# Attention and two MoE layers on one core: transposes five units behind the scores, products seven, and a fifth row buffer

## The chip, the cores and the metric

The kernel runs on one core of one Trainium2 chip. The metric is the device time of one execution in microseconds, the median of three runs. One execution was also recorded by the hardware profiler; it has a span (first to last instruction) and a time of its own.

## The reference, cut to what matters

```python
def _attn_ref(q, k, v, f):                       # 4 batches, 8 heads, 576 positions, head_dim 64
    scores = scale * np.matmul(q, k.transpose(0, 1, 3, 2))
    cum = np.cumsum(np.log(np.clip(f, 0.0001, 1.0)), axis=-1)
    decay = cum[:, :, :, None] - cum[:, :, None, :]
    scores = np.where(causal, -1000000000.0, scores + decay)
    attn = np.exp(scores - np.max(scores, axis=-1, keepdims=True))
    attn = attn / (np.sum(attn, axis=-1, keepdims=True) + 1e-09)
    return np.matmul(attn, v)

def reference(...):                              # 2304 tokens of width 512
    x = attn_out.transpose(0, 2, 1, 3).reshape(B * S, H * D)
    x = _moe_ref(x, w_gate, w_val, w_out, rms_g) # rms norm, silu(x@w_gate)*(x@w_val)@w_out, d_ff 1536
    return _moe2_ref(x, w_in, w_out)             # silu(x@w_in)@w_out, d_ff 2048
```

The MoE weights come as float64 and are cut to float32 on the chip.

## The kernel before

The program has two stages that hardly overlap on TensorE: attention first, then the two layers, each matmul of the latter split into three products of high and low parts (`terms`, L754).

Attention works on 16 pairs of heads (`Pair`), and in each pair on nine **units** (`Rows`): unit c holds query block c of both heads in 128 partitions and (c+1)*64 keys. The units of a pair are taken in the order of `ORDER`: c = 0, 1, 7, 2, 6, 3, 5, 4, 8, so that scores of 64, 128, 512, 192, 448, 256, 384, 320 and 576 keys (320 and 256 in two pieces) follow each other. For a unit:

- `bias` (GpSimd, L441 and L443) builds the decay in a tile `dt`;
- `scores` (L454) makes three matmuls into a PSUM bank `s` (four banks); VectorE adds the decay and takes the row extreme (L457) into a row buffer `pr`, which comes from a pool of `PRB` = 4 tiles of 128x576;
- `expo` (ScalarE, L470) applies the exponential in place;
- `turn` (L479, and L486 for the last block) transposes the row on TensorE in up to four pieces and moves it (L272 on ScalarE, L274 on VectorE) into a tile `g`;
- `use`, once in a pair, after unit c = 8, multiplies with v (L510): two groups of matmuls, results `t` and `o`. A matmul here has 64 columns: head j = 0 fills the lower half of the array's columns and j = 1 the upper half, and the loop writes them alternately.

A hand-written loop over steps sets the order of the program: at step s it writes the turn of unit s - `TURN`, the scores and the exponential of unit s, then the use of unit s - `USE`, then jobs that stand in a table by step: loads of a pair 12 steps before its first unit, transposes of k (L413) 6 steps and of q (L413) 5 steps before it, the tails of both (`operand_tails`, L424) 4 steps before it, the row sums of the decay (`load_sums`, L407) 8 steps before it. Jobs of the norm (L297 to L374) follow `USE`. A scheduler then orders each engine's instructions; where one is not ready by its reckoning, a later one of the program can go first. The order it writes is fixed: an engine executes it as it stands.

The weights of the layers are fetched (`weights`, L144) into one of two tiles `st`, cut to float32 into a tile `f`, and split into tiles `wh` and `wl` (`unit_plain`, L189 and L190), four buffers each. The first of them are prepared during attention; `spread` holds the n-th such work until after the exponential of unit 22, 40 and so on (`PLACE`, `STRIDE`).

Of the kernel before, what the change touches and what calls it, by code (L numbers as in the profile page):

```python
# [9 lines left out]
F32 = mybir.dt.float32  # L10
F32R = mybir.dt.float32r
I32 = mybir.dt.int32
# [6 lines left out]
P = 128  # L19
# [8 lines left out]
PRB = 4  # L28
# [3 lines left out]

ORDER = (0, 1, 7, 2, 6, 3, 5, 4, 8)

TURN = 4
USE = 6

WHEN = dict(load=-12, k=-6, sums=-8, q=-5, tails=-4)

# [21 lines left out]
def block_kernel(ctx: ExitStack, tc: tile.TileContext, q, k, v, f, w_gate, w_val, w_o1, rms_g, w_in, w_o2, ident_d, sel_d, hot_d, out):  # L61
    nc = tc.nc
    B, H, S, D = q.shape
    NT, DM = out.shape
# [4 lines left out]
    FULL = NC - 1  # L69
    TAIL = S - FULL * P  # L70
    SF = FULL * P
# [41 lines left out]
    wip = ctx.enter_context(tc.tile_pool(name="wip", bufs=4))  # L113
    wop = ctx.enter_context(tc.tile_pool(name="wop", bufs=3))
    stp = ctx.enter_context(tc.tile_pool(name="stp", bufs=2))
# [10 lines left out]
    def words(w):  # L126
        return (w, 1) if w.dtype == F32 else (w.bitcast(I32), 2)

    def weights(w, src, cols, key):

        n = DM
        wide = src.dtype != F32
        if cols is not None:
            src = src.rearrange("(c p) f -> p c f", p=P)
        if not wide or key in kept:
            if wide:
                nc.sync.dma_start(out=w, in_=kept[key])
            else:
                nc.sync.dma_start(out=w if cols is None else w.rearrange("p (c f) -> p c f", f=cols), in_=src)
            return  # L140
        wi = w.bitcast(I32)
        dst = stp.tile([P, 2 * n], I32, tag="st", name="st")
        pr = dst.rearrange("p (n t) -> p n t", t=2)
        nc.sync.dma_start(out=dst if cols is None else dst.rearrange("p (c f) -> p c f", f=cols), in_=src)  # L144
        top, low = pr[:, :, 1], pr[:, :, 0]
        nc.scalar.activation(out=w, in_=top.bitcast(F32), func=AF.Abs)  # L146
        nc.vector.tensor_scalar(out=w, in0=w, scalar1=FLOOR, scalar2=CAP, op0=ALU.max, op1=ALU.min)
        nc.vector.tensor_scalar(out=wi, in0=wi, scalar1=3, scalar2=0x3FFFFFF8, op0=ALU.logical_shift_left, op1=ALU.bitwise_and)
        nc.vector.scalar_tensor_tensor(out=wi, in0=top, scalar=-0x40000000, in1=wi, op0=ALU.bitwise_and, op1=ALU.bitwise_or)
        nc.vector.scalar_tensor_tensor(out=wi, in0=low, scalar=29, in1=wi, op0=ALU.logical_shift_right, op1=ALU.bitwise_or)  # L150
        kept[key] = dram.tile([P, n], F32, name="kept" + "_".join(map(str, key)))
        nc.sync.dma_start(out=kept[key], in_=w)
# [58 lines left out]
    def attention():  # L211
        exps, maxima = [], []
        with ExitStack() as st:
# [7 lines left out]
            prb = pool("prb", PRB)  # L221
# [154 lines left out]
            class Pair:  # L376
# [7 lines left out]
                def load(self, names="kqv"):  # L384
                    b, hp = self.b, self.hp
                    for nm in names:
                        src = {"k": k, "q": q, "v": v}[nm]
                        t = self.v if nm == "v" else nat.tile([P, NC, 2, D], F32, tag="nqk", name="n" + nm)
                        for j in range(2):
                            nc.sync.dma_start(out=t[:, :FULL, j], in_=src[b, 2 * hp + j, :SF].rearrange("(c p) d -> p c d", p=P))  # L390
                        for i, u in enumerate({"k": (), "q": (q, k), "v": (v,)}[nm]):
                            nc.sync.dma_start(out=t[i * TAIL : (i + 1) * TAIL, FULL], in_=u[b, 2 * hp : 2 * hp + 2, SF:].rearrange("j p d -> p j d"))
                        self.n[nm] = t

                def load_sums(self):

                    b, hp = self.b, self.hp
                    self.nct = t = dec.tile([P, S], F32, tag="ncb", name="ncb", bufs=2)
                    h = b * H + 2 * hp
                    if h == 0:  # L400
                        for w in (slice(0, HS), slice(HS, S)):
                            bp = bank(pss)[:, : w.stop - w.start]
                            nc.tensor.matmul(bp, lhsT=hot, rhs=n8[:, w], start=True, stop=True)
                            nc.scalar.activation(out=t[:, w], in_=bp, func=AF.Copy)
                    else:
                        for j in range(2):
                            nc.sync.dma_start(out=t[j * D : (j + 1) * D], in_=nc8d[h + j, :].partition_broadcast(D))  # L407

                def operand(self, nm):
                    n = self.n[nm]  # L410
# [11 lines left out]
                def operand_tails(self):  # L422
                    tl = bank(pss)
                    nc.tensor.transpose(tl[:, :P], self.n["q"][:, FULL].rearrange("p j d -> p (j d)"), ident)  # L424
                    for j in range(2):
# [2 lines left out]
                        hi, lo = (o[js, at_].rearrange("p (i w) -> p i w", w=w)[:, :, :D] for o in (self.oh, self.ol))  # L428
                        split(hi, lo, tl[js, :P].rearrange("p (i w) -> p i w", w=D))

            class Rows:


# [10 lines left out]

                def scores(self):
                    p, c, n = self.p, self.c, self.n
                    self.pr = prb.tile([P, S], F32, tag="pr", name="pr")
                    cs = slice(c * P, (c + 1) * P)
                    nms = []
                    for k0, w in ((0, n),) if n <= SF else ((0, G2 + D), (G2 + D, G2)):  # L450
                        at_ = QW + k0 + (D if n <= SF else 0)
                        sp = bank(pss)[:, :w]
                        for z, (l, r) in enumerate(((p.oh, p.oh), (p.oh, p.ol), (p.ol, p.oh))):
                            nc.tensor.matmul(sp, lhsT=l[:, cs], rhs=r[:, at_ : at_ + w], start=(z == 0), stop=(z == 2))  # L454
                        nm = sml.tile([P, 1], F32, tag="nm", name="nm", bufs=4)
                        ks = slice(k0, k0 + w)
                        reduced = nc.vector.tensor_tensor_reduce(  # L457
                            out=self.pr[:, ks], in0=sp, in1=self.dt[:, ks], op0=ALU.add, op1=ALU.min, scale=-SCALE, scalar=3.0e38, accum_out=nm
# [89 lines left out]
            nc8d = dram.tile([BH, S], F32, name="nc8d")  # L548
# [28 lines left out]
            nc.sync.dma_start(out=gcol, in_=rms_g.rearrange("(c p) -> p c", p=P))  # L577

            units, jobs = [], {}

            def at(step, *fns):
                jobs.setdefault(step, []).extend(fns)
# [18 lines left out]
            for n, p in enumerate(pairs):  # L601
                s = n * per
# [407 lines left out]
```

## Time and profile before

| | us |
|---|---|
| median of three runs (lowest, highest) | 1029.16 (1027.78, 1029.46) |
| the profiled execution's own time | 1031.82 |
| its span | 1030.0 |
| TensorE shown as busy in the span | 1015.3 |

The profile counts a matmul as busy from its start to a modelled end, so that short waits between matmuls hide in it. What a matmul takes in a stream is better read from start to start in the timeline.

### The profile page before, as it was taken

To read this page: it belongs to the slowest core of one execution; us is meant where nothing else is said; L and a number is where in the kernel's file an instruction comes from. 1 tells how busy PE (TensorE), PEld (TensorE's weight loads), DVE (VectorE), ACT (ScalarE), POOL (GpSimd) and SP (SyncE) were. 2 spreads that over 40 slices of the span, in tenths; PEclk is the share of its full clock that TensorE was granted. 3 is DMA by queue.
4 is the path that set the end of the run, shared out by engine and by line. 5 is a ranking of instruction groups with operands and counts; after the bars stand their busy time and mean duration, and the time that the engine had idled before them with its cause. 6 is when DMAs were issued, how large, how long until landed. Compare 5 with 4: busy or idle time off the path is not lost.

```text
span 1030.0 us, 16062 instructions
## 1 busy us (share of the span) xinstructions
PE 1015.3 (99%) x5457; PEld 849.5 (82%) x5457; DVE 758.2 (74%) x1519; ACT 566.5 (55%) x1193; POOL 395.9 (38%) x589
## 2 busy tenths in 40 slices
PE   8999999999999999999999999999999999999998
PEld 7877888878788888888888887888888888888887
DVE  6889887877788787876588768946666687366664
ACT  6998989884443332543544556564444465544441
POOL 7777656511011135331344633335533323222310
PEclk8999999999999999999999999999999999999999
DMA  6664433123645444230334222223322233121102
GB/s 143 169 185 124 124 93 95 36 63 111 191 148 188 133 151 153 72 123 31 108 123 138 82 62 82 83 82 113 113 83 82 82 123 144 42 62 62 51 1 82
DMA packets 114162, 106.40 MB, mean 103 GB/s; under 512 B 62896, under 2 KB 83792, under 8 KB 114080
## 3 DMA queue, kind: packets, MB, share of 16 engines
q1 hardware_dynamic: 112352, 102.23, 32.6%
q10 hardware_dynamic: 1728, 3.15, 1.0%
q8 instruction: 43, 0.70, 0.3%
q14 instruction: 39, 0.32, 0.1%
HBM read 79.59 MB, written 25.76 MB: 102 GB/s over the span
## 4 chain that ended last, share of the span: by engine, by line
PE 74%; DVE 3%; DMA 1%; ACT 1%; issue 1%; ACTq 0%; SPq 0%; DVEq 0%
PE t L754 38%; PE s L754 19%; PE x L754 16%; DMA c<-t 1%; DVE hl L673 1%; DMA st<-in_moe_w_in_dram 0%; PE o L510 0%; DVE t1l L673 0%; DVE xa L950 0%; PE s L297 0%; DVE b11l L673 0%; DVE c L771 0%; DVE c L885 0%; DVE xa L932 0%; PE t L479 0%
## 5 line engine op out<-in xcount | busy, mean ns | idle before, releaser
L203 POOL TENSOR_TENSOR wol<-c,woh 128x512 fp32r<-128x512 f32 x53 | 77.4, 1467 | 250.3 <-ACT woh L202 224.5
L673 DVE TENSOR_TENSOR hl<-c,hh 128x512 fp32r<-128x512 f32 (+1 forms) x140 | 107.5, 776 | 43.5 <-ACT hh L672 42.7
L165 POOL TENSOR_TENSOR f<-f 128x256 f32<-128x256 f32 x112 | 91.7, 840 | 110.4 <-DMA f<-keptb 64.3
L672 ACT ACTIVATE hh<-c 128x512 fp32r<-128x512 f32 (+1 forms) x140 | 79.6, 583 | 47.6 <-DVE c L885 42.5
L766 ACT ACTIVATE c<-t 128x512 f32<-128x512 f32 x84 | 49.6, 591 | 95.7 <-PE t L754 92.2
L441 POOL TENSOR_SCALAR dt<-ncb,c8t 128x64 f32<-128x64 f32 (+2 forms) x144 | 78.6, 547 | 36.2 <-DVE nm L457 28.3
L878 ACT ACTIVATE c<-c 128x512 f32<-128x512 f32 x66 | 41.6, 630 | 86.7 <-DVE c L771 86.7
L470 ACT ACTIVATE pr<-pr,nm 128x192 f32<-128x192 f32 (+3 forms) x144 | 80.2, 557 | 12.4 <-DVE nm L457 9.0
L457 DVE CUSTOM_DVE_ANT_0 pr<-s,dt 128x256 f32<-128x256 f32 (+7 forms) x160 | 70.1, 450 | 14.9 <-PE t L479 5.2
L190 POOL TENSOR_TENSOR wl<-f,wh 128x1024 fp32r<-128x1024 f32 x12 | 29.2, 2435 | 126.8 <-ACT wh L189 120.5
L171 DVE TENSOR_TENSOR wl<-f,wh 128x1024 fp32r<-128x1024 f32 (+1 forms) x48 | 59.9, 1254 | 21.3 <-ACT wh L170 21.1
L479 PE MATMUL t<-ident,pr 128*128 128x128 f32 x384 | 69.3, 280 | 3.9 <-ACT pr L470 3.0
L771 DVE TENSOR_TENSOR c<-t,c 128x512 f32<-128x512 f32 x60 | 41.2, 687 | 39.9 <-ACT c L766 26.3
L170 ACT ACTIVATE wh<-f 128x1024 fp32r<-128x1024 f32 (+1 forms) x56 | 54.4, 973 | 20.1 <-PE x L754 15.6
L950 DVE TENSOR_TENSOR xa<-x,xa 128x512 f32<-128x512 f32 x64 | 43.7, 683 | 29.3 <-PE x L754 29.2
L754 PE MATMUL s<-hh,woh 128*128 128x512 f32 (+1 forms) x172 | 64.2, 373 | 0.2 <-DVE xa L932 0.2
L754 PE MATMUL s<-hl,woh 128*128 128x512 f32 (+1 forms) x172 | 64.0, 372 | 0.0
L754 PE MATMUL s<-hh,wol 128*128 128x512 f32 (+1 forms) x172 | 64.0, 372 | 0.0
L950 DVE TENSOR_TENSOR xa<-s,xa 128x512 f32<-128x512 f32 (+1 forms) x63 | 43.1, 684 | 21.8 <-PE s L754 21.3
L146 ACT ACTIVATE f<-st 128x512 f32<-128x512 f32 x42 | 27.8, 667 | 54.5 <-DMA st<-in_moe_w_gate_dram 15.8
L932 DVE TENSOR_TENSOR xa<-s,xa 128x512 f32<-128x512 f32 (+1 forms) x72 | 45.5, 639 | 16.6 <-PE s L754 16.6
L878 ACT ACTIVATE c<-t 128x512 f32<-128x512 f32 (+1 forms) x74 | 37.7, 510 | 34.2 <-PE t L754 32.7
(247 smaller groups left out, 3238.9 us busy)
## 6 DMA issues: line engine op xcount, KB each, us to landing
st<-in_moe_w_out_dram SPq DMA_DIRECT2D x28, 512.0 KB, 3.6
st<-in_moe_w_in_dram SPq DMA_DIRECT2D x16, 512.0 KB, 3.9
f<-keptb SPq DMA_DIRECT2D x32, 256.0 KB, 2.6
st<-in_moe_w_gate_dram SPq DMA_DIRECT2D x12, 512.0 KB, 4.0
kepta<-f SPq DMA_DIRECT2D x24, 256.0 KB, 2.3
st<-in_moe_w_val_dram SPq DMA_DIRECT2D x12, 512.0 KB, 4.7
f<-kepta SPq DMA_DIRECT2D x24, 256.0 KB, 2.7
out_dram<-xa SPq DMA_DIRECT2D x17, 256.0 KB, 2.0
```

The costliest lines, as they stand in the source:

```text
L165: nc.gpsimd.tensor_tensor(out=out_, in0=x, in1=y, op=op)
L171: (nc.gpsimd if plain and i else nc.vector).tensor_tensor(out=lo[i][:, u], in0=f[i][:, u], in1=hi[i][:, u].bitcast(F32), op=ALU.subtract)
L203: nc.gpsimd.tensor_tensor(out=lo, in0=f, in1=hi.bitcast(F32), op=ALU.subtract)
L441: nc.gpsimd.tensor_scalar(out=dt, in0=p.nct[:, 0 if last else D :][:, :n], scalar1=c8t[:, c, p.i : p.i + 1], scalar2=1.0, op0=ALU.add, op1 ...
L457: reduced = nc.vector.tensor_tensor_reduce(out=self.pr[:, ks], in0=sp, in1=self.dt[:, ks], op0=ALU.add, op1=ALU.min, scale=-SCALE, scalar= ...
L470: e = nc.scalar.activation(out=pr, in_=pr, func=AF.Exp, bias=self.nm, scale=-1.0, accum_out=p.batch.sums[:, self.c, p.hp : p.hp + 1])
L479: nc.tensor.transpose(pt[:, jj * P : (jj + 1) * P], keys[:, jj * P : (jj + 1) * P], ident)
L672: nc.scalar.activation(out=hi, in_=src, func=AF.Copy)
L673: nc.vector.tensor_tensor(out=lo, in0=src, in1=hi.bitcast(F32), op=ALU.subtract)
L754: nc.tensor.matmul(ps, lhsT=l, rhs=r, start=start and z == 0, stop=stop and z == len(mms) - 1, skip_group_check=not (start and stop))
L878: act = nc.scalar.activation(out=hf, in_=a, func=AF.Silu)
L950: nc.vector.tensor_tensor(out=a, in0=ps, in1=a, op=ALU.add)
```

## The change

- `TURN` goes from 4 to 5 and `USE` from 6 to 7: a unit's transposes are written five steps after its scores, a pair's products seven steps after its last unit. The norm's jobs, which count from `USE`, move by one step too.
- Every fifth unit takes its row from a tile `fifth`, one of the four buffers `wl`, instead of from the pool of four; that `wl` buffer is free for weights only when the last such unit is transposed.
- The first two fetches of gate weights are written at steps 14 and 15 (`FETCH`) instead of after the exponential of unit 22; `weights` then takes the tile that was fetched.
- In `load_sums` the two row loads are held until the load of the q and k tails has been issued (`issue_after(self.held)`).

```diff
-TURN = 4
-USE = 6
+TURN = 5
+FETCH = 14
+USE = 7
...
+    def fetch_in(w, key, m):
+        w, s = words(w)
+        if s > 1:
+            fetched[key, m] = fetch(w[:, s * m * P : s * (m + 1) * P].rearrange("(c p) f -> p c f", p=P), s * P)
...
-        dst = stp.tile([P, 2 * n], I32, tag="st", name="st")
+        dst = fetched.pop(key) if key in fetched else fetch(src, cols)
...
-                        for j in range(2):
-                            nc.sync.dma_start(out=t[j * D : (j + 1) * D], in_=nc8d[h + j, :].partition_broadcast(D))
+                        with tc.issue_after(self.held):
+                            for j in range(2):
+                                nc.sync.dma_start(out=t[j * D : (j + 1) * D], in_=nc8d[h + j, :].partition_broadcast(D))
...
+            fifth = wip.tile([P, 4, G2], F32, tag="wl", name="pr").rearrange("p a f -> p (a f)")[:, :S]
+            shown = [0]
...
-                    self.pr = prb.tile([P, S], F32, tag="pr", name="pr")
+                    shown[0] += 1
+                    self.pr = fifth if shown[0] % (PRB + 1) == 0 else prb.tile([P, S], F32, tag="pr", name="pr")
...
+            for m in range(2):
+                jobs[FETCH + m] = [_p(fetch_in, w_gate, "a0", m)]
```

No instruction is added or removed on any engine; what changes is their order, up to the first MoE products. Line numbers of the changed kernel are higher: its L428 is L413 of before, L439 is L424, L473 is L454, L498 is L479, L505 is L486, L529 is L510, and L134 is L144.

**First place: the products of a pair, on TensorE, in the middle of attention.** Before: from the transposes of the next pair's q (L413 nq) past the scores of 256 keys to the products (L510) and the tails (L424).

```order
L413 MATMUL s<-ident,nq 128x128 x4
L479 MATMUL t<-ident,pr 128x128
L454 MATMUL s<-op0h 128x256
L454 MATMUL s<-op0l,op0h 128x256
L454 MATMUL s<-op0h,op0l 128x256
L510 MATMUL t<-g_1389,vn_140 64x256 x2
L510 MATMUL t<-g_1389,vn_140 64x128 x2
L510 MATMUL o<-g_1455,vn_140 64x320 x6
L510 MATMUL o<-g_1455,vn_140 64x192 x2
L510 MATMUL o<-gl_142,vn_140 64x64 x2
L424 MATMUL s<-ident,nq 128x128
```

The same place in the changed kernel, from the tails on:

```order
L439 MATMUL s<-ident,nq 128x128
L498 MATMUL t<-ident,pr 128x128
L529 MATMUL t<-g_1405,vn_140 64x256
L473 MATMUL s<-op0h 128x384
L473 MATMUL s<-op0l,op0h 128x384
L473 MATMUL s<-op0h,op0l 128x384
L529 MATMUL t<-g_1405,vn_140 64x256
L529 MATMUL t<-g_1405,vn_140 64x128 x2
L529 MATMUL o<-g_1472,vn_140 64x320 x6
L529 MATMUL o<-g_1472,vn_140 64x192 x2
L529 MATMUL o<-gl_142,vn_140 64x64 x2
```

The products now come after the tails, and their first matmul (j = 0) stands alone: three matmuls of the 384 scores lie between it and its partner (j = 1). Counted over the 16 pairs, the first product stands alone, ahead of scores, in 3 pairs before and in 14 pairs after; in 3 of the 14 the rest is cut once more by scores.

**Second place: the transposes of unit c = 8 (four and one), on TensorE, in a later pair.** Before, they stand right behind the scores of 512 keys:

```order
L454 MATMUL s<-op0h 128x512
L454 MATMUL s<-op0l,op0h 128x512
L454 MATMUL s<-op0h,op0l 128x512
L479 MATMUL t<-ident,pr 128x128 x4
L486 MATMUL t<-ident,pr 64x128
L454 MATMUL s<-op0h 128x192
```

In the changed kernel they stand after the scores of 192 keys and the transposes of the next pair's k (L428 nk):

```order
L473 MATMUL s<-op0h 128x512
L473 MATMUL s<-op0l,op0h 128x512
L473 MATMUL s<-op0h,op0l 128x512
L498 MATMUL t<-ident,pr 128x128 x3
L473 MATMUL s<-op0h 128x192
L473 MATMUL s<-op0l,op0h 128x192
L473 MATMUL s<-op0h,op0l 128x192
L428 MATMUL s<-ident,nk 128x128 x4
L498 MATMUL t<-ident,pr 128x128 x4
L505 MATMUL t<-ident,pr 64x128
```

Three matmuls of scores and four transposes of k now lie between the scores of 512 and the row that unit c = 8 left.

**Third place: the first gate weights on SyncE's queue.** Before, they stand behind the k of pair 4:

```order
L407 DMA ncb<-nc8d 64x576 x2
L390 DMA nk<-in_k_dram 128x4x64 x2
L144 DMA st<-in_moe_w_gate_dram 128x4x256 x2
L390 DMA nq<-in_q_dram 128x4x64 x2
L392 DMA nq<-in_q_dram 64x2x64
```

In the changed kernel they stand ahead of the k of pair 3:

```order
L422 DMA ncb<-nc8d 64x576 x2
L134 DMA st<-in_moe_w_gate_dram 128x4x256 x2
L402 DMA nk<-in_k_dram 128x4x64 x2
L402 DMA nq<-in_q_dram 128x4x64 x2
L404 DMA nq<-in_q_dram 64x2x64
```

The two fetches moved ahead by the loads of one pair.

## Rows read from the trace of the kernel before

**Rows 1.** Busy time by stretch: start:end, length, engines' busy us, clock, DMA

```profile
13.00:219.00 206.00, 199.75 (x1572) 165.66 (x1570) 170.30 (x619) 184.34 (x540) 134.85 (x355) 0.99 0.44 113
219.00:1030.00 811.00, 805.49 (x3843) 675.26 (x3843) 580.04 (x884) 374.98 (x641) 252.22 (x208) 1.00 0.31 100
```

**Rows 2.** Waits of TensorE's weight loads, 0 to 219: us, times, longest

```profile
PEld t L479 <- ACT pr L470: 8.2, 18, 0.9
PEld s L454 <- DVE nm L457: 3.0, 8, 0.5
```

**Rows 3.** Waits of TensorE's matmuls, 0 to 219

```profile
PE t L479 <- ACT pr L470: 3.0, 9, 0.5
```

**Rows 4.** Timeline of TensorE, 111.7 to 113.7: start, us, [idle before]

```profile
112.07 0.39 PE L454 MATMUL s<-op0l,op0h 128*128 128x512 f32 x1
112.30 0.40 PE L454 MATMUL s<-op0h,op0l 128*128 128x512 f32 x1
113.16 0.66 PE L479 MATMUL t<-ident,pr 128*128 128x128 f32 x4 [0.46 <-ACT pr L470]
113.65 0.27 PE L486 MATMUL t<-ident,pr 128*64 128x128 f32 x1
```

**Rows 5.** Timeline of TensorE, 62.4 to 66.3: products in one block

```profile
62.40 0.60 PE L413 MATMUL s<-ident,nq 128*128 128x128 f32 x4
...
63.06 0.28 PE L454 MATMUL s<-op0l,op0h 128*128 128x256 f32 x1
63.18 0.28 PE L454 MATMUL s<-op0h,op0l 128*128 128x256 f32 x1
63.39 0.87 PE L510 MATMUL t<-g,vn 128*64 128x256 f32 x8
64.09 2.11 PE L510 MATMUL o<-g,vn 128*64 128x320 f32 x16
66.03 0.28 PE L510 MATMUL o<-gl,vn 128*64 128x64 f32 x4
66.24 0.33 PE L424 MATMUL s<-ident,nq 128*128 128x128 f32 x1
```

**Rows 6.** Timeline of TensorE, 128.5 to 133.2: first product apart

```profile
128.51 0.60 PE L413 MATMUL s<-ident,nq 128*128 128x128 f32 x4
...
129.15 0.65 PE L510 MATMUL t<-g,vn 128*64 128x256 f32 x2
129.72 0.39 PE L454 MATMUL s<-op1h 128*128 128x256 f32 x1
129.95 0.28 PE L454 MATMUL s<-op1l,op1h 128*128 128x256 f32 x1
130.06 0.29 PE L454 MATMUL s<-op1h,op1l 128*128 128x256 f32 x1
130.28 0.65 PE L510 MATMUL t<-g,vn 128*64 128x256 f32 x4
130.56 0.43 PE L510 MATMUL o<-g,vn 128*64 128x320 f32 x1
...
133.13 0.33 PE L424 MATMUL s<-ident,nq 128*128 128x128 f32 x1
```

**Rows 7.** Timeline of TensorE, 103 to 142: where q of a pair is transposed

```profile
103.49 0.60 PE L413 MATMUL s<-ident,nq 128*128 128x128 f32 x4
...
115.23 0.60 PE L413 MATMUL s<-ident,nq 128*128 128x128 f32 x4
...
141.18 0.60 PE L413 MATMUL s<-ident,nq 128*128 128x128 f32 x4
```

**Rows 8.** Timeline of ScalarE, 213 to 215: end of attention

```profile
213.40 0.78 ACT L470 ACTIVATE pr<-pr,nm 128x576 f32<-128x576 f32 x1
214.08 0.19 ACT L470 ACTIVATION_READ_ACCUMULATOR pr<-pr,nm 128x1 f32 x1
214.17 0.48 ACT L272 ACTIVATE g<-t 128x384 f32<-128x384 f32 x1
```

**Rows 9.** Timeline of GpSimd, 219 to 240: second pair of weights

```profile
236.41 2.40 POOL L190 TENSOR_TENSOR wl<-f,wh 128x1024 fp32r<-128x1024 f32 x1 [6.31 <-ACT wh L189]
```

**Rows 10.** Timeline of TensorE, 218 to 219: first product of the layers

```profile
218.42 0.50 PE L754 MATMUL t<-b11h,wh 128*128 128x512 f32 x1
```

**Rows 11.** Timeline of SyncE's queue and, below, of ScalarE: first gate weights

```profile
34.72 1.06 SPq L144 DMA_DIRECT2D st<-in_moe_w_gate_dram  x2
...
40.15 0.68 ACT L146 ACTIVATE f<-st 128x512 f32<-128x512 f32 x1
```

More of the change, by code (lines that the diff above doesn't have):

```diff
@@ L127, in words, with fetch @@
         return (w, 1) if w.dtype == F32 else (w.bitcast(I32), 2)
+    fetched = {}
+    def fetch(src, cols):
+        dst = stp.tile([P, 2 * DM], I32, tag="st", name="st")
+        nc.sync.dma_start(out=dst if cols is None else dst.rearrange("p (c f) -> p c f", f=cols), in_=src)
+        return dst
+    def fetch_in(w, key, m):
+        w, s = words(w)
+        if s > 1:
+            fetched[key, m] = fetch(w[:, s * m * P : s * (m + 1) * P].rearrange("(c p) f -> p c f", p=P), s * P)
     def weights(w, src, cols, key):
@@ L141, in weights @@
         wi = w.bitcast(I32)
-        dst = stp.tile([P, 2 * n], I32, tag="st", name="st")
+        dst = fetched.pop(key) if key in fetched else fetch(src, cols)
         pr = dst.rearrange("p (n t) -> p n t", t=2)
-        nc.sync.dma_start(out=dst if cols is None else dst.rearrange("p (c f) -> p c f", f=cols), in_=src)
         top, low = pr[:, :, 1], pr[:, :, 0]
@@ L391, in load @@
                         for i, u in enumerate({"k": (), "q": (q, k), "v": (v,)}[nm]):
-                            nc.sync.dma_start(out=t[i * TAIL : (i + 1) * TAIL, FULL], in_=u[b, 2 * hp : 2 * hp + 2, SF:].rearrange("j p d -> p j d"))
+                            held = nc.sync.dma_start(out=t[i * TAIL : (i + 1) * TAIL, FULL], in_=u[b, 2 * hp : 2 * hp + 2, SF:].rearrange("j p d -> p j d"))
+                            if nm == "q":
+                                self.held = held.ins
                         self.n[nm] = t
```

## The prediction

> **What bounds the kernel now.** I read the busy time by stretch first. TensorE is the bound in both stages [rows 1]: in attention (13 to 219 us) it shows 199.75 us of 206, and in the layers 805.49 of 811. ScalarE follows in attention with 184.34 (89%), VectorE with 170.30. From the first MoE product on, the order of TensorE is nearly the same before and after, so the change of the time is the change of the moment when attention ends, and attention is a chain of TensorE work with short waits in it. What can be won are those waits; what can be lost is TensorE time that the new order costs.
>
> The waits came next. TensorE's weight loads waited 18 times, 8.2 us in all, for a unit's exponential before its transposes, and 3.0 us (8 times) for VectorE to free a score bank [rows 2]. Of the first kind the matmuls themselves show 3.0 us in 9 waits [rows 3]. The true loss lies between, since a matmul's modelled end covers part of a gap. The timeline shows one of the nine: the last matmul of the 512 scores starts at 112.30 and the transposes of unit c = 8 at 113.16, 0.86 us on, where the same matmul before it took 112.30 - 112.07 = 0.23 [rows 4]. So 0.63 us were lost where 0.46 are shown as idle, 1.37 times as much.
>
> Then I read the place where the change cuts the products with v, in both forms that it already has before. In 12 of the 16 pairs the block is whole [rows 5]; in 3 its first product (j = 0) stands alone, ahead of scores [rows 6] (the last pair's block is cut otherwise). From the transposes of q to the tails both hold the same instructions: whole 66.24 - 62.40 = 3.84 us, cut 133.13 - 128.51 = 4.62 us. The cut costs 0.78 us. The reason is to be seen in the rows: a whole block runs both halves of the columns at once, eight matmuls of the first group in 64.09 - 63.39 = 0.70 us; alone, the two records of the first half take 129.72 - 129.15 = 0.57 us with the other half empty, and the block that follows still needs 133.13 - 130.28 = 2.85 us, exactly what the whole one needs (66.24 - 63.39), because the second half has lost nothing of its work. A pair with a whole block took 115.23 - 103.49 = 11.74 us from one transposing of q to the next, the pair with the cut 141.18 - 128.51 = 12.67 [rows 6, 7].
>
> **The change, part by part.**
>
> *Transposes one unit later.* Removes waits for the exponential. The place of [rows 4] is the clearest: a wait of under a us, while the second place of the order now puts three scores and four transposes of k before the same transposes. I price all of these waits: nine at 3.0 x 1.37 = 4.1 us, and 0.1 us each for the nine that only the loads show, 5.0 us together, taken as gone. Bounds: 3.0 [rows 3] and 8.2 [rows 2]. Value -5.0.
>
> *Products after the next scores.* `USE` = 7 puts the products behind the scores of unit c = 5 (384 keys) in the program, and the scheduler lets only the first of them slip ahead. 14 blocks are cut instead of 3: 11 x 0.78 = +8.6 us. Where three of them are cut a second time, there is another way in and out of the block (the scores' last matmul takes 0.21 us ahead of products, 63.39 - 63.18, where its neighbour takes 0.12, 63.18 - 63.06 [rows 5]) and one more odd product: 0.3 each, +0.9, an estimate from these rows. Nothing hides it: the engine that pays is the one that bounds. Lower bound: only the work of the lone half counts, as the time of the first two product pairs in the whole block would have it, 0.70 x 256 / (256 + 128) = 0.47 each, 11 x 0.47 = 5.2. Upper bound: each second cut costs as much as a first, 14 x 0.78 = 10.9.
>
> A rule speaks to this term. The row has a lone half of 0.57 us and a whole cost of 0.78 [rows 6]. The Trainium skill, "TensorEngine Tiling (Array Packing)", section Key Properties, says that tiles work independently and that a change of the tiling mode drains TensorE. By independence alone a cut would cost only the lone half's stream, and the sum of the edit would be the lower bound; with the drains it would be about the upper value. The trace agrees with both parts: 0.57 of stream with its way in, and 0.21 beyond it. I go by the measured pair.
>
> *The end.* One more unit is left to transpose after the last scores. Its eviction takes some 0.5 us on ScalarE, which runs without a break there [rows 8]; four transposes take 0.5 us on TensorE (113.65 - 113.16 [rows 4]), partly in waits. +0.5, bounds 0 and 1.0.
>
> *Score banks.* The 384 scores now come right behind the tails and meet their bank sooner, while later scores have had a slower TensorE ahead of them. I let a third of the 3.0 us [rows 2] go: -1.0. Bounds: -3.0, and +3.0 if as much is added.
>
> *Fifth buffer.* With five units between scores and transposes, five buffers are what four were for four: the next user still waits for the transposes written just ahead of it. Its price would be weights that come late; the fourth `wl` tile is filled only at 236.41 [rows 9], after attention has ended at 218.42 [rows 10], so the buffer is free again before it is wanted. 0. Without that cover it would be the 2.40 us that the split takes.
>
> *Gate weights at step 14.* Two fetches go ahead of the k, q and v of pair 3. Before they were issued at 34.72 and first read at 40.15 [rows 11], 5.4 us later, with the k of a pair behind them. Loads are written six units before their transposes, and a unit takes 206 / 144 = 1.4 us [rows 1], so 8.6 us stand against a delay of about 5.4 at most. 0; bounds 0 and +2.
>
> *Row loads held.* They only change places with loads that stand beside them on SyncE's queue. 0.
>
> The sum: -5.0 + 8.6 + 0.9 + 0.5 - 1.0 = +4.0 us. On the profiled execution's own 1031.82 that gives 1035.8; that execution was 2.7 us above the median of the runs, 1029.16, so the median becomes **1033.2 us**, 0.4% slower. A change of 0.2% (2.1 us) is about what a measurement of this kernel can tell from none.
>
> **The rivals.**
>
> *Faster: the cut falls into time that was lost anyway.* The scheduler lets the first product ahead because it reckons the 384 scores not ready. If they are not ready on the chip either, the lone half fills a wait, and costs only its drains, 0.21 each: 11 x 0.21 = 2.3. With the waits for exponentials and two thirds of the bank waits gone: 2.3 - 5.0 - 2.0 + 0.5 = -4.2, so 1025.0. It breaks even where a cut costs (5.0 + 1.0 - 0.5 - 0.9) / 11 = 0.42 us, and is faster below that. For it: the bank waits of [rows 2] are real. Against it: in [rows 6] the scores follow the lone product with no wait shown. Chance 0.2.
>
> *Same: the two halves balance.* At the lower bound for the cuts (5.2) and 5.0 of waits won, the remaining terms (+0.5, -1.0) leave 1028.9. Or ScalarE at 89% sets a pair's length, and TensorE's order moves nothing: 1029.2. Against the latter: exponentials are waited for 18 times in 144 units [rows 2], not at each. Chance 0.25.
>
> *Slower by more:* waits won only by 3.0, cuts at 10.9, banks +3.0, end 1.0: +11.9, 1041.1. It needs all bounds at once; 0.05. The forecast itself, between 1031.3 and 1038.5: 0.5.
>
> **How the numbers follow.** The likeliest case gives 1033.2. Slower by over 0.2% takes the forecast and the worse case: 0.55; same 0.25; faster 0.2. The range reaches from 1026.0, which leaves out about half of the faster case, to 1038.5, which leaves out the worse one and some of the forecast's upper part: 0.8 inside.
>
> **What would show it.** In the changed profile the weight loads before the transposes should wait less than 2 us for the exponential. In the timeline, 14 blocks should show two records of the first product, about 0.57 us, then scores, then a block of 2.85. The pair of 11.74 us [rows 7], which had one wait of 0.63 [rows 4], should take 11.74 - 0.63 + 0.78 = 11.9. The first MoE product should start near 222.4 instead of 218.42 [rows 10], and the layers should again take 811 us. I am wrong if lone products show up inside waits, if the waits for exponentials persist, or if the stage of the layers changes its length.

## The result, and the profile after

The changed kernel took 1039.83 us (median of four runs, 1038.48 to 1041.38), the kernel before in the same runs 1029.05 (1027.78 to 1029.46): a ratio of 1.010, 95% interval 1.0084 to 1.0116, or 10.8 us slower. The forecast had the sign right (+4.0) and the size wrong by a factor of 2.7; 1039.83 lies above the range of 1026.0 to 1038.5. In the comparisons below, single executions that were disturbed (of 1678 us and more) are left out; the profiled execution of one kernel, `e13_before_nosums`, was such a one, so its trace isn't read.

The profiled execution took 1038.48 us, with a span of 1036.7, 6.7 us more than before. First the busy time by stretch, cut at the first product of the layers, as in [rows 1]:

```profile
13.00:227.00 214.00, 204.28 (x1563) 169.97 (x1561) 168.51 (x616) 184.17 (x536) 136.48 (x352) 1.00 0.42 109
227.00:1037.00 810.00, 804.94 (x3844) 675.48 (x3843) 579.06 (x883) 375.58 (x642) 252.83 (x208) 1.00 0.31 101
```

Attention takes 8 us more, the layers as long as before (810 us, 811). The first product of the layers, in the timeline of TensorE, starts 8.3 us later than in [rows 10] (222.4 was forecast):

```profile
226.76 1.33 PE L776 MATMUL t<-b11h,wh 128*128 128x512 f32 x4
```

The beginning hides some of the loss: in this execution the second pair's q was transposed at 13.50 us, in the profiled one of before at 16.68. This comes with the execution, not with the kernel, and the granted clock shows it (the last figure but two; before, then after):

```profile
12.00:17.00 5.00, 5.00 (x20) 4.47 (x20) 2.26 (x11) 3.05 (x10) 4.92 (x14) 0.50 0.59 151
12.00:17.00 5.00, 4.37 (x31) 3.55 (x29) 3.96 (x15) 4.47 (x14) 4.83 (x14) 1.00 0.55 142
```

TensorE was granted half its clock there (1.2 GHz) in the one, the whole (2.4 GHz) in the other, after being busy for 4.78 and 4.54 of the 5 us from 5 to 10. Two variants of the kernel before that share its first pair had the transposing at 13.68, at a clock of 1.00 in that stretch, and at 16.49, at 0.50. From that transposing to the first product of the layers, which I call **the stage** below, it is 226.76 - 13.50 = 213.26 us after and 218.42 - 16.68 = 201.74 before: +11.5. The one before has its first 1.7 us still at half clock, so that the true difference may be up to 0.9 us larger, an estimate.

The waits of TensorE's weight loads, 0 to 227 us (us in total, times, longest), which answer to [rows 2]:

```profile
PEld s L439 <- issue: 5.7, 4, 1.7
PEld s L473 <- issue: 4.7, 11, 0.7
PEld s L439 <- PE s L473: 3.4, 4, 1.0
...
PEld s L473 <- DVE op0l L280: 2.1, 5, 0.5
PEld t L498 <- ACT gl L284: 1.7, 3, 0.9
...
PEld t L498 <- ACT pr L489: 0.8, 1, 0.8
```

The waits for exponentials are gone, as forecast: 0.8 us once, where there were 8.2 us in 18 waits. At the top stands a line that [rows 2] doesn't have at all: the transposes of the tails (L439) wait, 9.1 us in eight places. "issue" and "PE s L473" don't say for what. The timeline of TensorE does, in the pair whose k is transposed at 114.66:

```profile
113.78 0.40 PE L473 MATMUL s<-op0h,op0l 128*128 128x512 f32 x1
114.02 0.49 PE L498 MATMUL t<-ident,pr 128*128 128x128 f32 x3
...
114.66 0.60 PE L428 MATMUL s<-ident,nk 128*128 128x128 f32 x4
115.10 0.60 PE L498 MATMUL t<-ident,pr 128*128 128x128 f32 x4
115.79 0.30 PE L505 MATMUL t<-ident,pr 128*64 128x128 f32 x1
115.84 0.45 PE L473 MATMUL s<-op0h 128*128 128x448 f32 x1
...
116.54 0.60 PE L428 MATMUL s<-ident,nq 128*128 128x128 f32 x4
116.97 0.27 PE L498 MATMUL t<-ident,pr 128*128 128x128 f32 x1
117.00 0.36 PE L473 MATMUL s<-op0h 128*128 128x256 f32 x1
117.20 0.28 PE L473 MATMUL s<-op0l,op0h 128*128 128x256 f32 x1
117.32 0.28 PE L473 MATMUL s<-op0h,op0l 128*128 128x256 f32 x1
119.08 0.30 PE L439 MATMUL s<-ident,nq 128*128 128x128 f32 x1 [1.48 <-issue]
119.21 0.27 PE L498 MATMUL t<-ident,pr 128*128 128x128 f32 x1
119.42 0.65 PE L529 MATMUL t<-g,vn 128*64 128x256 f32 x2
119.99 0.44 PE L473 MATMUL s<-op0h 128*128 128x384 f32 x1
```

ScalarE and, below, VectorE in the same stretch:

```profile
116.00 0.72 ACT L489 ACTIVATE pr<-pr,nm 128x512 f32<-128x512 f32 x1
116.62 0.20 ACT L489 ACTIVATION_READ_ACCUMULATOR pr<-pr,nm 128x1 f32 x1
116.71 0.63 ACT L214 ACTIVATE woh<-f 128x512 fp32r<-128x512 f32 x1
117.23 0.45 ACT L489 ACTIVATE pr<-pr,nm 128x192 f32<-128x192 f32 x1
117.57 0.20 ACT L489 ACTIVATION_READ_ACCUMULATOR pr<-pr,nm 128x1 f32 x1
117.67 0.59 ACT L279 ACTIVATE op1h<-s 128x512 fp32r<-128x512 f32 x1
```

```profile
118.28 0.69 DVE L280 TENSOR_TENSOR op1l<-s,op1h 128x512 fp32r<-128x512 f32 x1 [1.66 <-ACT op1h L279]
118.89 0.61 DVE L476 CUSTOM_DVE_ANT_0 pr<-s,dt 128x448 f32<-128x448 f32 x1
```

The reader is to count score banks. There are four, and here they are taken in turn: k's transposes (114.66), the scores of 448, q's transposes (116.54), the scores of 256, and then the tails, which so get the bank of k again. That bank is free when k has been split: the high part on ScalarE at 117.67, behind two exponentials and a weight, then the low part on VectorE from 118.28 to 118.97. The tails start at 119.08. In 10 of the 14 pairs from the third on they start less than 0.15 us after the low part of k has ended (in three more 0.8 to 0.9 us after it, in one before it), in none of before; there the median is 2.35 us, because the whole block of products, 2.85 us [rows 5], stood between the scores of 256 and the tails. The change moved the tails ahead of that block and took their cover away.

VectorE's order has a part in it. Above it stands idle for 1.66 us until k's high part is there, while the scores of 448 (last matmul at 116.33) wait to be read behind k's low part, and hold another bank. In the kernel before, at the same place (k's transposes at 114.08), it read the scores of 448 first:

```profile
115.54 0.62 DVE L457 CUSTOM_DVE_ANT_0 pr<-s,dt 128x448 f32<-128x448 f32 x1
116.51 1.28 DVE L268 TENSOR_TENSOR op1l<-s,op1h 128x512 fp32r<-128x512 f32 x2 [0.34 <-ACT op1h L267]
```

Of the 15 pairs after the first, VectorE reads the scores of 448 ahead of k's low part in 10 before and in 2 after.

### The profile page after: what moved, and what is told of

It reads as the page before. It is cut to its first block, busy times and chain, and to the rows that moved or that the text cites. A ratio compares the mean times of both kernels' runs of the same rounds, so it can differ in the third digit from the quotient of the medians.

```text
span 1036.7 us, 16053 instructions
## 1 busy us (share of the span) xinstructions
PE 1019.1 (98%) x5457; PEld 854.0 (82%) x5457; DVE 756.4 (73%) x1519; ACT 567.7 (55%) x1193; POOL 399.1 (38%) x589
## 4 chain that ended last, share of the span: by engine, by line
PE 92%; DVE 4%; ACT 2%; issue 2%; POOL 0%; ACTq 0%; DVEq 0%
PE t L776 38%; PE s L776 19%; PE x L776 16%; PE s L473 6%; PE t L498 4%; PE o L529 3%; PE t L529 2%; PE s L428 1%; ACT pr L489 1%; PE s L383 1%; PE t L264 0%; PE s L309 0%; DVE wl L183 0%; DVE hl L695 0%; PE s L439 0%
## 5 line engine op out<-in xcount | busy, mean ns | idle before, releaser
L177 POOL TENSOR_TENSOR f<-f 128x256 f32<-128x256 f32 x112 | 91.5, 838 | 106.5 <-DMA f<-keptb 62.4
L489 ACT ACTIVATE pr<-pr,nm 128x192 f32<-128x192 f32 (+3 forms) x144 | 80.0, 557 | 10.8 <-DVE nm L476 9.4
L498 PE MATMUL t<-ident,pr 128*128 128x128 f32 x384 | 68.1, 278 | 1.3 <-ACT gl L284 0.9
```

Source lines behind the costliest of these rows:

```text
L177: nc.gpsimd.tensor_tensor(out=out_, in0=x, in1=y, op=op)
L489: e = nc.scalar.activation(out=pr, in_=pr, func=AF.Exp, bias=self.nm, scale=-1.0, accum_out=p.batch.sums[:, self.c, p.hp : p.hp + 1])
L498: nc.tensor.transpose(pt[:, jj * P : (jj + 1) * P], keys[:, jj * P : (jj + 1) * P], ident)
```

## The experiments

Each kernel was timed beside the kernel before on the same chip; a ratio is to that, and the us beside it are the difference of the medians. Executions of one kernel lie some 3 us apart, so a difference of medians is good to 1 or 2 us only; where it and the ratio say different things, the ratio with its interval counts. For the waits I use an account of my own: from the start of one matmul of TensorE's records to the start of the next I take off what the same step takes in the stream where nothing waits (0.11 us for a transpose, 0.09 more where the kind of matmul changes, and so on); what is left over, if over 0.04 us, is a wait of the matmul that comes late. These waits are estimates. "Products" is the time from start to start that L510 (L529) takes.

```
us, one profile each     stage   products  waits: rows'   tails  384     all
                                           transposes            scores
before                   201.74  47.6      7.8            0.1    0.0     11.8
changed                  213.26  54.4      4.0            8.4    0.6     13.9
e1_whole                 212.79  47.4      4.6            7.6    5.2     20.5
e2_whole_tails3          209.50  45.7      7.2            0.1    6.0     18.5
e3_cut_tails3            212.86  54.2      6.9            0.1    0.0     13.2
e4_nofetch               214.26  54.4      4.9            8.6    0.0     15.0
e5_use6                  206.81  48.7      5.2            0.2    0.6     13.9
e6_turn4_use7            206.28  48.7      5.4            1.8    1.2     13.0
e7_norm_back             214.75  54.7      5.2            7.6    0.5     14.6
e8_k_earlier             207.36  49.7      6.6            0.4    1.8     11.8
e9_before_whole          202.59  45.8      7.8            0.1    0.6     14.3
e10_before_cut           208.25  54.4      7.7            0.1    0.0     10.3
e11_before_k7            206.51  45.8      8.6            0.0    0.0     16.9
e12_k7_whole             207.75  46.5      6.2            0.8    5.1     15.4
e14_changed_nosums       210.50  54.4      2.9            6.4    0.0     11.8
e15_changed_kcopy        206.81  48.2      3.3            2.9    0.5     13.6
e16_before_kcopy         205.07  45.8      9.4            0.0    0.0     15.6
```

The profiled executions of `e1_whole` and `e12_k7_whole` show a granted clock of 0.50 for some 3.4 us inside the stage (from 82.6 and 77.9 us on), which can lengthen theirs by up to 1.7 us.

**Are the cuts the loss?** Two theories: the cut blocks cost what the forecast says (theirs was the largest term), or the tails' bank does. Four kernels, the first with every block of products held behind the 384 scores:

```diff
-                def use(self):
+                def use(self, after=None):
                     if self.c == ORDER[-1]:
-                        outs = [self.use_group(gi) for gi in range(2)]
+                        with ExitStack() if after is None else tc.issue_after(after):
+                            outs = [self.use_group(gi) for gi in range(2)]
...
-                    units[s - USE].use()
+                    units[s - USE].use(units[s].scored if s < N else None)
```

> The changed kernel, with each pair's products held until the scores written before them have been issued, so that all 16 blocks are whole; the tails stay ahead of the products. Theory (two costs: cut blocks, and tails that wait for their score bank): 14 cuts less at 0.78 us take 11 us from 1039.8, so 1027 to 1031; the tails still start within 0.15 us of the end of the k split on VectorE, with 7 to 9 us of waits in all. Rival A (only the tails' wait costs; the lone product fills time that is lost anyway): 1037 to 1041. Rival B (the time went to the fetch, the held loads or the fifth buffer): 1037 to 1041.

Measured: 1.0103 (1.0086 to 1.0120), +11.3 us. Without one cut the kernel is as slow as with 14. The products' own time fell back to 47.4 us, and the 7 us saved turned up as waits, in the loads' list:

```profile
PEld s L473 <- DVE nm L476: 6.9, 14, 1.0
PEld s L439 <- PE s L473: 4.3, 5, 1.1
PEld s L439 <- issue: 4.0, 3, 1.3
```

The lone products had been filling time in which the 384 scores had no bank: in 10 of 15 pairs these now start 0.06 us after VectorE has read the scores of 448. The second kernel is the first with the tails a step later, behind the products, where they stood before:

```diff
-WHEN = dict(load=-12, k=-6, sums=-8, q=-5, tails=-4)
+WHEN = dict(load=-12, k=-6, sums=-8, q=-5, tails=-3)
```

> As the run before, and the tails of q and k one unit later (3 units ahead instead of 4), so that they stand behind the products. Theory: the tails' wait of 8 us goes too, 1019 to 1023, which beats the kernel before by 6 to 10 us; the tails start 1 us or more after the k split. Rival A: also about 1030. Rival B: no better than 1029.

Measured: 1.0080 (1.0067 to 1.0093), +8.2 us. The tails no longer wait (0.1 us), but now the 384 scores are the fifth to ask for a bank, k's, and they wait 6.0 us. The third adds a lone first product in 15 blocks again (`lead=True` writes the first matmul alone):

```diff
+                led = 0 <= s - USE < N and units[s - USE].c == ORDER[-1]
+                if led:
+                    units[s - USE].use_group(0, lead=True)
                 if 0 <= s < N:
-                    units[s].scores()
+                    with tc.issue_after(units[s - USE].led[1]) if led else ExitStack():
+                        units[s].scores()
```

> The order of the run before on TensorE, except that the first product of 15 blocks is put alone ahead of the 384 scores. Theory: 15 cuts at 0.78 us, 11.7 us over the run before (1031 to 1035). Rival A: no slower than the run before by more than 3 us (15 x 0.21).

Measured: 1.0095 (1.0079 to 1.0111), +10.8 us; by the medians 15 cuts cost 2.7 us more than none, 0.18 us each, though the products' own time grew by 54.2 - 45.7 = 8.5. The intervals of the two kernels overlap, so that the 2.7 are not clear of nothing; they are clear of the 11.7 that were expected. The fourth undoes the early fetch and the held row loads:

```diff
-                        with tc.issue_after(self.held):
+                        with ExitStack():
...
-            for m in range(2):
-                jobs[FETCH + m] = [_p(fetch_in, w_gate, "a0", m)]
```

> The changed kernel with the gate weights fetched as before and the row loads not held; the order on TensorE is that of the changed kernel. Theory: 1038 to 1041, the same as the changed kernel. Rival B (early fetch or held loads delay the loads of a pair): 1036 or less.

Measured: 1.0114 (1.0099 to 1.0129). These parts of the change cost nothing, as forecast.

**Which of the two steps?** The changed kernel with `USE` = 6, the kernel before with `USE` = 7 alone, the changed one with the norm's jobs where they were (`AFTER`), and the changed one with k's transposes a step earlier (`k=-7`), so that more time lies between them and the tails. In this order:

```diff
-USE = 7
+USE = 6
...
-USE = 6
+USE = 7
...
-AFTER = (2, 3, 3, 4, 1, 1)
+AFTER = (1, 2, 3, 4, 1, 1)
...
-WHEN = dict(load=-12, k=-6, sums=-8, q=-5, tails=-4)
+WHEN = dict(load=-12, k=-7, sums=-8, q=-5, tails=-4)
```

> The changed kernel with USE back at 6: transposes five units behind, fifth buffer, early fetch and held loads stay; the products stand ahead of the tails again, with 4 cut blocks. Theory (now: the products' block was the cover behind which ScalarE and VectorE freed the bank of k; without it the tails, or whatever takes that bank, wait, and a cut mostly falls into that wait): 1024 to 1028, faster than the kernel before by the waits for exponentials, with no wait at the tails. Rival C (ScalarE's load sets the length of a pair, whatever TensorE's order): 1028 to 1032. Rival D (the later transposes push ScalarE's evictions into the split of k): 1035 or more.

> The kernel before with USE = 7 alone. Theory: the products behind the tails cost by themselves: 1034 to 1040. Rival D: 1028 to 1031, no different from the kernel before.

> The changed kernel with the norm's jobs put back to the steps at which they stood before (the first two offsets of AFTER one less). Theory: pairs with work of the norm lose 1 to 2 us each less in 7 such pairs if that shift costs: 1031 to 1035; if the shift is free, 1038 to 1041.

> The changed kernel with the transposes of k one unit earlier (7 units ahead of a pair instead of 6), so that ScalarE and VectorE have a unit more to free its bank. Theory: most of 8 us of waits go, 1031 to 1036. Rival C: 1038 to 1041.

Measured: `TURN` = 5 without `USE` = 7 (the fifth buffer, the early fetch and the held loads stay in) 1.0026 (1.0014 to 1.0038), +1.8 us; `USE` = 7 alone 1.0036 (1.0023 to 1.0050), +2.8; with the norm moved back 1.0113 (1.0095 to 1.0130), so the norm's place is free; with k a step earlier 1.0042 (1.0027 to 1.0057), +5.0. By the ratios the two steps alone make 2.7 and 3.7 us, 6.4 together, and both at once 10.3: they work on each other, by some 4 us, which the intervals leave open between 1.5 and 6.5. In the traces the stage is 5.1 and 4.5 us longer than before with one step and 11.5 with both, which leaves 2 us to their meeting. So more than half of the loss comes with one step or the other by itself.

The tails' wait is what needs both: 0.2 and 1.8 us with one step, 8.4 with both. In the records, k's bank is free 2.27 us after its transposes before (mean of 14 pairs) and the tails ask for it after 4.64. `TURN` = 5 makes the first later (3.06 alone, 2.68 with `USE` = 7), `USE` = 7 the second earlier (2.03 alone, 2.86 with `TURN` = 5, waits included). By these means `USE` = 7 alone should have made the two meet as well. It did not, because there the tails mostly got another bank:

```profile
59.95 0.62 DVE L457 CUSTOM_DVE_ANT_0 pr<-s,dt 128x448 f32<-128x448 f32 x1
60.91 1.28 DVE L268 TENSOR_TENSOR op1l<-s,op1h 128x512 fp32r<-128x512 f32 x2 [0.33 <-ACT op1h L267]
```

```profile
60.63 0.33 PE L424 MATMUL s<-ident,nq 128*128 128x128 f32 x1
61.75 0.41 PE L454 MATMUL s<-op0h 128*128 128x384 f32 x1 [0.35 <-DVE op1l L268]
```

VectorE has read the scores of 448 at 60.57, the tails start at 60.63, 0.3 us before k's low part is even begun, and the 384 scores wait for k's bank instead. So it is in 8 of 15 pairs: the four banks are not always taken in turn. In 12 of 15 pairs, here and in the changed kernel, the tails start within 0.15 us after VectorE has freed the first of the two banks.

`TURN` = 5 alone isn't faster either, since products now follow the last transposes by one unit and wait for their eviction, in the loads' list:

```profile
PEld t L529 <- ACT gl L284: 4.3, 9, 0.8
```

**What does a cut cost, and k a step earlier, in the kernel before?** The kernel before with its three cuts made whole, with a lone product in 15 blocks ahead of the 256 scores, and with k a step earlier; and the changed kernel with k earlier and all blocks whole, by the edits shown above:

> The kernel before with every pair's products held behind the scores of 256 keys, so that its three cut blocks are whole too. Theory (a cut costs 0.78 us where the products have no other wait around them): 3 x 0.78 us less, 1 to 3 us below the kernel before. Rival C (ScalarE sets the length of a pair): no difference over 0.5 us.

> The same with the first product put alone ahead of the 256 scores in 15 pairs; nothing else in TensorE's order differs from the run before. Theory: 15 x 0.78 = 11.7 us above the run before. If the lone half falls into waits here too: 2 to 4 us above. Rival C: no difference over 1 us.

> The kernel before with the transposes of k one unit earlier; the three cuts go with it. Theory: at most what the three cuts cost, 0 to 3 us below the kernel before, since its tails wait for no bank; if k's bank holds up others there too, 3 us or more below.

> The changed kernel with the transposes of k one unit earlier and all blocks whole. Theory: neither tails' waits nor cuts are left, and the waits for exponentials are gone: 1025 to 1030. Rival C: about 1033 to 1036, as with k earlier alone, the time moving from cuts into other waits.

Measured: 0.9992 (0.9981 to 1.0003), 1.0046 (1.0033 to 1.0060), 1.0040 (1.0027 to 1.0053) and 1.0050 (1.0037 to 1.0063). In the kernel before, 15 cuts cost 1035.37 - 1029.93 = 5.4 us, 0.36 each (0.25 to 0.49 by the intervals of the ratios), half of the 0.78 that was forecast: whole, the 256 scores wait 3.7 us for a bank, cut 0.2. Moving k earlier costs the kernel before 4 us; with k there, the change itself adds nothing that can be told apart. Made whole on top, the blocks again give nothing back: the products get 3.2 us shorter, and the 384 scores wait 5.1 us instead of 1.8.

**Is it ScalarE's load?** k's high part waits in ScalarE's queue, and one rival of the forecast was that this engine sets the length of a pair. In two kernels the row sums were left out of the exponential (they are set to 1, and the output is not divided by them):

```diff
-                    e = nc.scalar.activation(out=pr, in_=pr, func=AF.Exp, bias=self.nm, scale=-1.0, accum_out=...)
+                    e = nc.scalar.activation(out=pr, in_=pr, func=AF.Exp, bias=self.nm, scale=-1.0)
```

> The kernel before, with the row sums left out of the exponential (no accumulated output, the sums are set to 1, so the output is not divided by them); TensorE's order is that of the kernel before to a few places. ScalarE loses 144 readings of the accumulator of some 0.19 us, about 27 us of the 184 it shows in attention. Theory (TensorE and its bank waits bound, ScalarE only through the moment at which k's high part is made): waits for exponentials shrink, stage some 3 to 6 us shorter, ratio 0.994 to 0.998. Rival (ScalarE's queue sets the length of a pair): 15 to 25 us shorter, ratio 0.976 to 0.986. A second rival (ScalarE plays no part): ratio 0.999 to 1.001.

> The changed kernel with the row sums left out in the same way. Theory: k's high part comes sooner after k's transposes, the tails' wait falls from 8.4 us to under 3, and this kernel stands only 2 to 6 us above the other one without sums, instead of 10.8. Rival (the waits come from the order on TensorE and VectorE alone): tails still wait 6 us or more and the difference stays at 9 to 12 us. Rival (ScalarE sets the length of a pair in both): both fall by 15 to 25 us and the difference is gone.

Measured: 1.0008 (0.9998 to 1.0018) and 1.0087 (1.0072 to 1.0103). The kernel before gained nothing, the changed one 0.13% beside its 1.010, which the intervals cannot tell from nothing. The work taken away was less than I had written, since a reading of the accumulator overlaps its neighbours (in the rows above the next instruction starts 0.09 us after it, not 0.20). The busy time by stretch shows it, 25 to 215 us of the changed kernel with and, below, without the sums (ScalarE is the fourth figure):

```profile
25.00:215.00 190.00, 180.91 (x1387) 152.86 (x1386) 150.29 (x549) 163.61 (x478) 126.15 (x323) 1.00 0.44 113
```

```profile
25.00:215.00 190.00, 182.49 (x1404) 153.80 (x1403) 152.61 (x555) 155.84 (x359) 128.42 (x329) 1.00 0.44 113
```

So 7.8 us less of ScalarE, and the tails still waited 6.4 us (8.4), k's high part started 1.11 us after k's transposes instead of 1.31, and the distance between the two kernels stayed at 1039.04 - 1030.53 = 8.5 us. My theory (2 to 6 us) missed; ScalarE's load sets neither the pair nor most of this wait.

**Is it the bank?** The last two let k's bank go sooner without touching the place of its transposes: ScalarE copies the bank, and the split reads the copy. The copy ends 0.6 and 0.7 us sooner after k's transposes (changed kernel, kernel before) than the low part did in the twins with whole blocks.

```diff
-                        split(self.oh[:, QW + D :], self.ol[:, QW + D :], ps)
+                        kc = n[:, :FULL].rearrange("p c j d -> p (c j d)")
+                        nc.scalar.activation(out=kc, in_=ps[:, :SF], func=AF.Copy)
+                        split(self.oh[:, QW + D :], self.ol[:, QW + D :], kc)
```

> The changed kernel with k's transposes copied from their score bank by ScalarE into the tile that held k (free by then) and split from there, so that the bank is let go after one ScalarE instruction instead of ScalarE's and then VectorE's; nothing is left out, ScalarE does 16 more copies of some 0.6 us. The scheduler then leaves the products whole, all 14 in one piece behind the 384 scores, as in the run with whole products (1.0103). Theory (the loss is the wait for k's bank): the bank is free about 0.7 us sooner in each pair, the tails' wait falls from 7.6 us to under 2, ratio 1.000 to 1.005. Rival (the chain through the split of the tails or of q sets the pace, the bank was only where it showed): the wait moves on and the ratio stays above 1.008.

> The kernel before with the same copy, the control: its tails never wait for the bank, so an earlier release gains nothing. Theory: ratio 0.999 to 1.002, the copy being hidden (ScalarE has room, as the run without row sums showed). Rival (ScalarE's extra work shows): 1.003 or more.

Measured: changed 1.0063 (1.0046 to 1.0079), +5.7 us; control 1.0038 (1.0023 to 1.0052), +3.4. The same edit made the changed kernel faster than its twin with whole blocks (`e1_whole`, +11.3) and the kernel before slower than its twin (`e9_before_whole`, -0.2). The distance between changed and before, both with whole blocks (in the changed kernel with the copy three blocks are cut in the middle), is 11.3 + 0.2 = 11.5 us with k's bank held through the split (each against the kernel before) and 1036.21 - 1033.90 = 2.3 us with the copy. So the changed kernel waits for score banks, and a bank that goes sooner gives time back. Two things stay open. The 9 us between the two distances are the price of the bank only if the copy costs both kernels the same otherwise, which isn't shown. And with the copy VectorE reads the scores of 448 ahead of k's low part in all 15 pairs of both kernels (without it in 10 before and 2 after), so that the earlier release and VectorE's order were not tried apart. Tails wait 2.9 us instead of 7.6, 384 scores 0.5 instead of 5.2; their waits now name the copy (L431), in the changed kernel's list of loads' waits:

```profile
PEld s L441 <- ACT nk L431: 3.9, 7, 0.9
```

The control expected the copy to be hidden and was wrong: its rows' transposes wait 9.4 us instead of 7.8, most likely since the exponentials that stand behind the copy in ScalarE's queue come later; the loads' list:

```profile
PEld t L481 <- ACT pr L472: 9.5, 22, 0.8
```

No kernel here is faster than the kernel before beyond its interval; `e9_before_whole` can't be told apart from it.

## Why the prediction was right in sign and wrong in size

- **Waits for exponentials, -5.0: the mechanism held.** The loads' wait fell from 8.2 to 0.8 us. By my account all waits of the rows' transposes fell by 3.8 us (7.8 to 4.0), not 5.0: some now wait for an eviction (the 1.7 us for `gl` above). At the place of [rows 4], the four transposes now follow k's without a gap (115.10 after 114.66), and the fifth comes 0.2 us late.
- **Score banks, -1.0, bounds -3.0 and +3.0: the step that failed.** I let bank waits shrink because the order gave scores more time, and asked only who uses a bank for scores. The tails use one too. The order shown ahead of the prediction has them leave the place behind the products and stand right behind the 256 scores; I didn't count back four banks from there to k, nor look up when k's bank is let go and what VectorE does before that. The tails' wait is 8.3 us more in the trace; by the pair of kernels with the copy it is about 9 us (11.5 - 2.3), if the copy costs both the same. Either is about three times my upper bound. The other bank waits and those behind the norm did shrink, by about 2.4 us.
- **Cuts, +8.6 and +0.9: the own time is right, the price is not.** In the timeline of a cut block after:

```profile
105.63 0.65 PE L529 MATMUL t<-g,vn 128*64 128x256 f32 x2
106.20 0.44 PE L473 MATMUL s<-op1h 128*128 128x384 f32 x1
...
106.92 0.65 PE L529 MATMUL t<-g,vn 128*64 128x256 f32 x4
107.20 0.43 PE L529 MATMUL o<-g,vn 128*64 128x320 f32 x1
...
109.77 0.66 PE L498 MATMUL t<-ident,pr 128*128 128x128 f32 x4
```

  The lone product takes 106.20 - 105.63 = 0.57 us and the rest 109.77 - 106.92 = 2.85, as in [rows 6], and 14 blocks are cut. The products' time grew by 6.8 us. The Trainium skill, "TensorEngine Tiling (Array Packing)", section Key Properties, has tiles work independently, so that the second half's work stays where it was; the 2.85 agrees. But what reaches the end is 0.36 us a cut in the kernel before and, by the medians, 0.18 beside the bank wait, since the lone half runs while the scores behind it have no bank yet. That was the mechanism of the rival "the cut falls into time lost anyway" (it broke even at 0.42 us, which the 0.25 to 0.49 of the kernel before leave open). It was right about where a cut falls; the tails' new wait outweighed it. The rival "slower by more" gave 1041.1, near the result, by other terms: the waits won at their least and every cut at its dearest.
- **The end, +0.5.** From the start of the last scores' last matmul to the first product of the layers it is 7.28 us, before 6.45: +0.8.
- **Fifth buffer, gate weights, held loads, 0.** Undoing the fetch and the held loads changed nothing; the fourth `wl` is filled 17.7 us after the first product of the layers, before 18.0 [rows 9, 10].
- **The pair of 11.74 us** [rows 7] took 12.27 where 11.9 was forecast.

The sign was luck. With 0.36 us a cut, 11 cuts make 4.0 us, and my own sum would have been -5.0 + 4.0 + 0.9 + 0.5 - 1.0 = -0.6 us, about nothing. It came out slower by a term that was too dear, and the kernel was slower by waits that the sum didn't have.

Of the trace's +11.5 us in the stage, tails make +8.3, the products' own time +6.8, rows' transposes -3.8, other waits about -2.4. The remaining 2.6 us, the end among them, I can't place one by one. That the rival "ScalarE sets a pair's length" is out follows from the kernels without sums. Why `TURN` = 5 lets k's high part start later (1.31 to 1.73 us after k's transposes, before 0.91) stays open: it follows more instructions in ScalarE's queue, but taking 7.8 us of work from that queue only brought 0.2 back.

## What to carry to other kernels

When an order changes, go through every user of a rotating set of buffers, small ones too: count back as many users as there are buffers, and ask when the one found there lets go, what long block stood between as cover, and what stands ahead of the release in the queue of the engine that frees it. Then see in the trace which buffer was really taken: the turn can be another. A wait that two moves make together need not show in either of them alone. And a matmul put into a gap shows its full time in a sum of TensorE work, though the end pays only what the gap didn't cover; time it by a kernel that adds it alone.

## What the hardware showed that I had not expected

- The tails' wait for a bank that VectorE frees was shown as "issue" (5.7 us) or under the scores of the same engine (3.4), and in no row under L280, the instruction that ends 0.1 us ahead of the late matmul.
- The Trainium skill, "Perfetto Trace Analysis", section Matmuls, advises that groups rotate through PSUM banks so that an eviction overlaps the next group. Four banks are in use here, and the tails still lost 8.4 us: the split, two engines in a row, holds k's bank for 2.68 us after its transposes, and its turn comes round sooner.
- ScalarE gave up 7.8 us of its busy time and the changed kernel gained 0.13%, within the intervals; the same engine with 16 more copies cost the kernel before 3.4 us. What stood ahead of an instruction in the queue seems to count for more than how much work there was; that was not tried by itself.
